# Order of the products on TensorE: second products alternate upper and lower weights, first products go 1, 3, 2, 4

## The chip, the cores and the metric

The kernel runs on one core of one Trainium2 chip. The metric is device time in microseconds (us) of one execution. Before the change the median of 3 runs is 1911.17 us (1909.87 to 1912.69).

## What is computed

An attention with 49 agents in the middle, followed by a two-layer network on every token. The inputs are `q`, `k`, `v` of 4 batches x 12480 tokens x 128, `agents` of 4 x 49 x 128, `w_in` of 128 x 2048 and `w_out` of 2048 x 128, all in double or single precision on the host's side.

```python
a2k = sm(agents, k)              # softmax(scale * agents @ k.T)
agent_v = a2k @ v                # 49 x 128 for each batch
q2a = sm(q, agents)              # tokens x 49
x = (q2a @ agent_v)              # the attention's output, 49920 tokens x 128
h = np.maximum(x @ w_in, 0.0)    # 49920 x 2048
out = h * h @ w_out              # 49920 x 128
```

## The kernel before

The network's first layer is folded into the attention: for each batch a table `aw` = `agent_v @ w_in` (49 rows, kept as an upper part `aw_hi` and a small remainder in `aw_ex`) is made, and the hidden layer of 480 tokens is then a product of `aw` with the softmax weights of these tokens (`w` and `x`). The 2048 hidden columns are cut into 16 chunks of 128. The unit of the main loop is a pair of two double chunks, that is four chunks of 128 columns for one group of 480 tokens; there are 416 such units, called pairs below. For each pair TensorE (PE) does this:

- Four **first products**, `h<-w,aw_hi`: the weights are four neighbouring pieces of 128 columns of `aw_hi`, and the moving operand is each time the same `w` (128 x 480). They write two tiles of PSUM, `hs[0]` and `hs[1]`, of two banks each. The pool `ps_h` has three such tiles, so `hs[0]` of a pair takes the tile that was `hs[1]` two pairs before, and `hs[1]` takes the tile that was `hs[0]` one pair before.
- Four small products, `h<-x,aw_ex`, 19 rows each, which add the remainder to the four outputs and run at the same time in four strips of the array.
- Up to sixteen small products of background work (`psa<-...`), which stand between the next four, in some pairs.
- Four products of the half-precision remainder `o<-g_lo,wo_half` and eight **second products** `o<-g_hi,wo_hi` and `o<-g_hi,wo_lo`, for the pair that came two before. All twelve add into one PSUM tile `o`. The eight take the four tiles `g_hi` (the squared hidden values, 128 x 480) each with an upper and a lower part of `w_out`.

Meanwhile ScalarE (ACT) takes `r` = relu of `hs[0]` and of `hs[1]` (two instructions, line 464) and squares both into `g_hi`. VectorE (DVE) multiplies `gg<-r,h` out of `hs[0]`, which is the last reader of `hs[0]`, then `h<-r,h` in place in `hs[1]` and `g_lo<-h,g_hi` out of it, which is the last reader of `hs[1]`. GpSimd (POOL) makes the other half of `g_lo` at line 493.

The order on PE, ACT and DVE is fixed by hand: the helper `queued` (line 464 is the call in it) chains each instruction behind the one issued before it on its engine. What comes first in the Python loops comes first on the engine. The background work of the next batch (scores, softmax, tables) is dealt out between these steps by `step` and `share`. The lines that the change touches are the loop over the four first products in `first` and the list `todo` in `second`.

Of the kernel before, what the change touches and what calls it, by code (L numbers as in the profile page):

```python
# [43 lines left out]
def agent_attention_relu2(ctx: ExitStack, tc: tile.TileContext, qT, kT, v, agT, w_in, w_out, outT):  # L44
    nc = tc.nc
# [35 lines left out]
    for base in (NA, -NA):  # L81
        nc.gpsimd.affine_select(
            out=quad.rearrange("p h a -> p (h a)"), in_=quad.rearrange("p h a -> p (h a)"),
# [4 lines left out]
    wo_hi = const.tile([P, NCH, C], F32R, name="wo_hi")  # L88
    wo_lo = const.tile([P, NCH, C], F32R, name="wo_lo")
# [106 lines left out]
    state = {}  # L196
# [264 lines left out]
    def queued(issue, eng, *args, **kw):  # L461

        with tc.issue_after(chain[eng]) if eng in chain else ExitStack():
            ins = issue(*args, **kw)  # L464
        chain[eng] = ins.ins
        return ins

    def first(k):

        g, i = divmod(k, SLOTS)  # L470
        j, c = divmod(i, NP)
        b = g // NB
        w, x = weights[g][j]
        hs = [ps_h.tile([P, 2, 512], F32, name="h") for _ in range(2)]
        outs = [h[:, n, :G] for h in hs for n in range(2)]
        for n, out in enumerate(outs):
            cs = slice((2 * c + n) * P, (2 * c + n + 1) * P)
            queued(nc.tensor.matmul, nc.tensor, out, state[b]["hi"][:, cs], w, start=True, stop=False)

        with tc.high_priority():  # L480
            for t, out in enumerate(outs):
                rows = slice(t * 32, t * 32 + NL)
                queued(nc.tensor.matmul, nc.tensor, out, state[b]["lo"][rows, c // 2, :], x[rows, :], start=False, stop=True)
        r = ffn.tile([P, 2, 2, G], F32, name="r", bufs=RB)
        hi = ffn.tile([P, 2, 2, G], F32R, name="g_hi", bufs=HB)
        gg = ffn.tile([P, 2, G], F32, name="gg", bufs=GB)
        queued(nc.scalar.activation, nc.scalar, r[:, 0], hs[0][:, :, :G], AF.Relu, scale=2.0**-26)
        queued(nc.vector.tensor_mul, nc.vector, gg, r[:, 0], hs[0][:, :, :G])
        queued(nc.scalar.activation, nc.scalar, r[:, 1], hs[1][:, :, :G], AF.Relu, scale=2.0**-26)
        queued(nc.scalar.activation, nc.scalar, hi, r, AF.Square, scale=2.0**13)  # L490
        lo = ffn.tile([P, 2, G], F16, name="g_lo", bufs=LB)
        for n in range(2):
            chain[nc.gpsimd] = nc.gpsimd.tensor_sub(lo[:, n, :], gg[:, n, :], hi[:, 0, n, :].bitcast(F32)).ins  # L493
        parts[k] = hi[:, 0], lo
        yield
        queued(nc.vector.tensor_mul, nc.vector, hs[1][:, :, :G], r[:, 1], hs[1][:, :, :G])
        yield
        lo = ffn.tile([P, 2, G], F16, name="g_lo", bufs=LB)
        queued(nc.vector.tensor_sub, nc.vector, lo, hs[1][:, :, :G], hi[:, 1].bitcast(F32))
        parts[k + 1] = hi[:, 1], lo  # L500
# [3 lines left out]
    def share(n, new):  # L504
        if n == 1:
            calls = [fill.pop(0) for _ in range(min(len(fill), NT // 2 if many[0] else NT))]
            due[:] = [[], [], [], []]
            for at in range(len(calls)):
                due[2 + at % 2 if new else 1 + at % 3].append(None)
            for d in due:  # L510
                for at in range(len(d)):
                    d[at] = calls.pop(0)
        for call in due[n]:
            call()
# [5 lines left out]
    def second(k):  # L520
        g, i = divmod(k, SLOTS)
        j, c = divmod(i, NP)
        if c == 0:
            acc[0] = ps_t.tile([P, 512], F32, name="o", tag=f"turn{turn[0]}")
        o = acc[0]
        pair = [(c + d, *parts.pop(k + d)) for d in range(2)]
        todo = [(wo_half[:, 2 * c + n, :], lo[:, n, :]) for c, hi, lo in reversed(pair) for n in range(2)]
        for c, hi, lo in pair:
            todo += [(w[:, 2 * c + n, :], hi[:, n, :]) for w in (wo_hi, wo_lo) for n in range(2)]
        for n, (w, y) in enumerate(todo):  # L530
            if 0 < n < 4:
                share(n, i % NP == 0)
            queued(
                nc.tensor.matmul, nc.tensor, o[:, :G], w, y,
                start=(i % NP == 0 and n == 0), stop=(c == NP - 1 and n == len(todo) - 1),
            )
        return (g, j, o) if c == NP - 1 else None
# [7 lines left out]
    def background(b):  # L545

        kt = load_keys(b, 0, kv, "kt")
        for i in range(NB):
            nxt = load_keys(b, i + 1, kv, "kt") if i + 1 < NB else load_values(b, 0, kv, "vt")
            yield from scores(b, i, kt)  # L550
            yield 0.5
            kt = nxt
        yield from maxima(b)
        yield
        vt = load_values(b, 1, kv, "vt")
        ready = yield from weighed(b, 0, kt, False, nc.gpsimd)
        for i in range(NB):
            yield PACE
            nxt = load_values(b, i + 2, kv, "vt") if i + 2 < NB else None
            more = (yield from weighed(b, i + 1, vt, False, nc.gpsimd)) if i + 1 < NB else None  # L560
            yield from gathered(b, i, *ready)
            vt, ready = nxt, more
        yield
        yield from tables(b)
# [73 lines left out]
    for k in range(total + LAG):  # L638
        if k < total:
            g, c = divmod(k, SLOTS)  # L640
            b, i = divmod(g, NB)
            if k > LAG and (k - LAG) % NP == 0:
                turn[0] = 1 - turn[0]
            if i == 0 and c == 0 and b + 1 < B:
                todo = background(b + 1)
# [26 lines left out]
            if k % 2 == 0:  # L672
                begun = first(k)
                next(begun)
        if k % 2 == 0:
            ready = second(k - LAG) if k >= LAG else flush()
            marks.append([chain[nc.scalar], chain[nc.vector], chain[nc.gpsimd]])
            next(begun, None)
            if ready:
                out(*ready)  # L680
        else:
            next(begun, None)
# [32 lines left out]
```

## Time and profile before

| | |
|---|---|
| median of 3 runs | 1911.17 us |
| lowest, highest | 1909.87, 1912.69 us |
| the profiled execution, its own time | 1909.7 us |
| its span, first to last instruction | 1907.9 us |
| mean granted TensorE clock | 0.991 |
| PE busy | 1872.2 us (98%) |
| ACT busy | 1677.9 us (88%) |
| DVE busy | 1659.8 us (87%) |
| POOL busy | 1354.4 us (71%) |

A busy share says how much of the span an engine had an instruction running. Matmuls are pipelined, so the records of one overlap those of the next: a matmul of 480 columns has a record of about 0.38 us, while the next starts about 0.2 us after it. What a matmul costs is therefore read from the distance of two starts, not from its duration. The weights of a matmul are loaded by a separate record (PEld), which runs while the matmul before it streams.

### The profile page before, as it was taken

The numbers are of one execution on the slowest core, as the hardware profiler recorded it, in microseconds if no ns is written. First come the engines' busy times: TensorE is split into PE (matmuls) and PEld (weight loads), VectorE is DVE, ScalarE is ACT, GpSimd is POOL, SyncE is SP. The second block draws the span as 40 slices with busy tenths as digits, with TensorE's granted clock in tenths as the row PEclk, the third lists the DMA queues.
The fourth block names the chain that finished last, engine by engine and source line by source line (L and its number), as shares of the span: only waits on it lengthen the run. The fifth ranks groups of instructions, "written<-read, shape, count | busy, mean of one in ns | idle before, by whom it ended". The sixth has DMA issues, their size and how long they took to land.

```text
span 1907.9 us, 31019 instructions
## 1 busy us (share of the span) xinstructions
PE 1872.2 (98%) x10778; PEld 1396.9 (73%) x10778; DVE 1659.8 (87%) x1936; ACT 1677.9 (88%) x1613; POOL 1354.4 (71%) x1288
## 2 busy tenths in 40 slices
PE   7799999999999999999999999999999999999999
PEld 7577777777777777777767877777767777777776
DVE  6987888888987888888998788888899989999897
ACT  3577899998887899999888789999889999999997
POOL 2665688987665688988666568989767676767675
PEclk8899999999999999999999999999999999999999
DMA  9343222221123322222112322222111111111110
GB/s 300 108 124 97 78 84 71 77 79 52 60 65 97 102 79 72 78 78 62 59 45 87 103 67 71 83 73 64 56 44 55 52 51 53 47 52 46 58 36 29
DMA packets 67025, 142.81 MB, mean 75 GB/s; under 512 B 9304, under 2 KB 45812, under 8 KB 66868
## 3 DMA queue, kind: packets, MB, share of 16 engines
q1 hardware_dynamic: 66868, 140.83, 24.4%
q8 instruction: 85, 1.39, 0.3%
q14 instruction: 72, 0.59, 0.1%
HBM read 81.17 MB, written 25.56 MB: 56 GB/s over the span
## 4 chain that ended last, share of the span: by engine, by line
PE 86%; DVE 6%; DMA 3%; issue 2%; ACT 2%; POOL 1%; SPq 0%; POOLq 0%; DVEq 0%; ACTq 0%
PE o L464 52%; PE h L464 24%; PE psa L464 10%; DVE gg L464 2%; DMA raw<-in_w_in 1%; DVE g_lo L464 1%; DMA ahead<-in_v 1%; ACT r L464 1%; DVE h L464 1%; POOL g_lo L493 1%; DVE aw_half L362 1%; ACT g_hi L464 1%; DMA ahead<-in_kT 0%; DMA raw<-in_w_out 0%; DVE ob L464 0%
## 5 line engine op out<-in xcount | busy, mean ns | idle before, releaser
L493 POOL TENSOR_TENSOR g_lo<-gg,g_hi 128x480 f16<-128x480 f32 x832 | 998.4, 1222 | 417.2 <-ACT g_hi L464 257.5
L464 ACT ACTIVATE r<-h 128x960 f32<-128x960 f32 x832 | 763.5, 967 | 117.5 <-PE h L464 59.8
L464 ACT ACTIVATE g_hi<-r 128x1920 fp32r<-128x1920 f32 x416 | 754.2, 1813 | 30.8 <-ACT r L464 1.1
L464 DVE TENSOR_TENSOR g_lo<-h,g_hi 128x960 f16<-128x960 f32 x416 | 479.9, 1154 | 124.9 <-ACT g_hi L464 95.1
L464 PE MATMUL o<-g_hi,wo_hi 128*128 128x480 f32 x1664 | 568.9, 423 | 0.0
L464 DVE TENSOR_TENSOR gg<-r,h 128x960 f32<-128x960 f32 x416 | 479.4, 1152 | 84.8 <-ACT r L464 80.0
L464 PE MATMUL o<-g_lo,wo_half 128*128 128x480 f16 x1664 | 516.8, 370 | 0.6 <-POOL g_lo L493 0.5
L464 PE MATMUL o<-g_hi,wo_lo 128*128 128x480 f32 x1664 | 495.9, 379 | 0.0
L464 DVE TENSOR_TENSOR h<-r,h 128x960 f32<-128x960 f32 x416 | 480.4, 1155 | 1.0
L464 PE MATMUL h<-w,aw_hi 128*128 128x480 f32 x1664 | 435.2, 382 | 12.4 <-DVE gg L464 5.1
L464 PEld LDWEIGHTS h<-w,aw_hi 128*128 128x128 f32 x1664 | 311.9, 189 | 69.2 <-DVE gg L464 13.1
L464 PEld LDWEIGHTS o<-g_hi,wo_hi 128*128 128x128 f32 x1664 | 314.6, 189 | 50.0 <-issue 0.8
L464 PEld LDWEIGHTS o<-g_hi,wo_lo 128*128 128x128 f32 x1664 | 312.5, 188 | 48.6
L464 PEld LDWEIGHTS <-wo_half 128*128 128x128 f16 x1664 | 172.0, 112 | 149.4 <-issue 97.0
L464 PE MATMUL h<-x,aw_ex 19*128 19x480 f16 x1664 | 159.5, 373 | 0.0
L464 PEld LDWEIGHTS <-aw_ex 19*128 19x128 f16 x1664 | 41.8, 91 | 138.7 <-issue 138.3
L464 PEld LDWEIGHTS psa<-ag,qt 128*120 128x120 f32 x816 | 127.6, 187 | 6.8 <-issue 0.4
L464 PE MATMUL psa<-ag,qt 128*120 128x49 f32 x816 | 118.2, 249 | 0.0
L398 POOL TENSOR_TENSOR e<-e,z 120x392 f32<-120x392 f32 x52 | 44.2, 850 | 60.9 <-PE h L464 33.8
L266 POOL TENSOR_TENSOR vs<-vt,vs 120x1024 fp32r<-120x1024 f32 x39 | 85.8, 2200 | 0.0
L464 PEld LDWEIGHTS psa<-ag,kt 128*120 128x120 f32 x624 | 78.1, 184 | 5.8 <-DVE ob L464 3.2
L464 PE MATMUL psa<-ag,kt 128*120 128x49 f32 x624 | 76.8, 260 | 0.1
(152 smaller groups left out, 1121.4 us busy)
## 6 DMA issues: line engine op xcount, KB each, us to landing
qt<-in_qT SPq DMA_DIRECT2D x52, 480.0 KB
out_T<-ob SPq DMA_DIRECT2D x104, 240.0 KB
vt<-in_v SPq DMA_DIRECT2D x39, 483.8 KB
kt<-in_kT SPq DMA_DIRECT2D x39, 480.0 KB
w<-ph SPq DMA_DIRECT2D x102, 91.9 KB
w<-y SPq DMA_DIRECT2D x102, 91.9 KB
x<-half SPq DMA_DIRECT2D x416, 17.8 KB
ahead<-in_v SPq DMA_DIRECT2D x13, 483.8 KB
```

Of the source, the lines that this page charges most:

```text
L266: last[nc.gpsimd] = nc.gpsimd.tensor_sub(vs[:, :, C + 1 : 2 * C + 1], vt[:, :, :C], vs[:, :, :C].bitcast(F32))
L362: cut = nc.vector.tensor_copy(half, lo.bitcast(F32)).ins
L398: nc.gpsimd.tensor_mul(e, e, z.broadcast_to([TP, NT, NA]))
L464: ins = issue(*args, **kw)
L493: chain[nc.gpsimd] = nc.gpsimd.tensor_sub(lo[:, n, :], gg[:, n, :], hi[:, 0, n, :].bitcast(F32)).ins
```

## The change

Two loops are written in another order. In `first` the four products of a pair are issued for `n` in 0, 2, 1, 3 and no longer 0, 1, 2, 3; each keeps its own weights and output. In `second` the eight products of a pair are issued as upper, lower on the first `g_hi` tile, then upper, lower on the next, and no longer upper on two tiles and then lower on the same two.

```diff
-        for n, out in enumerate(outs):
+        for n in (0, 2, 1, 3):
             cs = slice((2 * c + n) * P, (2 * c + n + 1) * P)
-            queued(nc.tensor.matmul, nc.tensor, out, state[b]["hi"][:, cs], w, start=True, stop=False)
+            queued(nc.tensor.matmul, nc.tensor, outs[n], state[b]["hi"][:, cs], w, start=True, stop=False)
...
-            todo += [(w[:, 2 * c + n, :], hi[:, n, :]) for w in (wo_hi, wo_lo) for n in range(2)]
+            todo += [(w[:, 2 * c + n, :], hi[:, n, :]) for n in range(2) for w in (wo_hi, wo_lo)]
```

On PE, early in the main loop, the second products of one pair and the first products of the next stand in this row before (`o` is the sum in PSUM; `h_1413` is `hs[0]` of the new pair and `h_1414` its `hs[1]`; what an instruction waits for stands in brackets):

```order
L464 MATMUL o_1240<-g_hi_1281,wo_hi_103 128x480 [waits Activation_49]
L464 MATMUL o_1240<-g_hi_1281,wo_hi_103 128x480
L464 MATMUL o_1240<-g_hi_1281,wo_lo_104 128x480 x2
L464 MATMUL o_1240<-g_hi_1281,wo_hi_103 128x480 x2
L464 MATMUL o_1240<-g_hi_1281,wo_lo_104 128x480 x2
L464 MATMUL h_1413<-w0_1150,aw_hi_764 128x480 [waits DVE_49]
L464 MATMUL h_1413<-w0_1150,aw_hi_764 128x480
L464 MATMUL h_1414<-w0_1150,aw_hi_764 128x480 [waits DVE_49]
L464 MATMUL h_1414<-w0_1150,aw_hi_764 128x480
```

And the same place on PE now:

```order
L464 MATMUL o_1240<-g_hi_1281,wo_hi_103 128x480 [waits Activation_49]
L464 MATMUL o_1240<-g_hi_1281,wo_lo_104 128x480
L464 MATMUL o_1240<-g_hi_1281,wo_hi_103 128x480
L464 MATMUL o_1240<-g_hi_1281,wo_lo_104 128x480
L464 MATMUL o_1240<-g_hi_1281,wo_hi_103 128x480
L464 MATMUL o_1240<-g_hi_1281,wo_lo_104 128x480
L464 MATMUL o_1240<-g_hi_1281,wo_hi_103 128x480
L464 MATMUL o_1240<-g_hi_1281,wo_lo_104 128x480
L464 MATMUL h_1413<-w0_1150,aw_hi_764 128x480 [waits DVE_49]
L464 MATMUL h_1414<-w0_1150,aw_hi_764 128x480 [waits DVE_49]
L464 MATMUL h_1413<-w0_1150,aw_hi_764 128x480
L464 MATMUL h_1414<-w0_1150,aw_hi_764 128x480
```

Upper and lower weights now alternate one by one, and the first write to `hs[1]`, with its wait for DVE, moved from the third place among the first products to the second.

The rows of ACT and SP are the same. On DVE and POOL only the first two or three pairs after the start differ, where the decoding of `w_out` (lines 117 and 118) and the first softmax (lines 388 to 397) are fitted between the pairs' steps. On DVE:

```order
-L464 TENSOR_TENSOR gg<-r,h 128x960
 L117 TENSOR_SCALAR rest<-raw 128x256
-L388 TENSOR_REDUCE m<-psa 120x8
+L118 SCALAR_TENSOR_TENSOR rest<-raw,rest 128x256
 L117 TENSOR_SCALAR rest<-raw 128x256
-L464 TENSOR_TENSOR h<-r,h 128x2x480
+L464 TENSOR_TENSOR gg<-r,h 128x960
 L118 SCALAR_TENSOR_TENSOR rest<-raw,rest 128x256
-L390 TENSOR_TENSOR e<-psa,m 120x392
```

There the first `gg` moved behind three steps of the decoding, and the softmax's `m` and `e` moved further back.

## Rows read from the trace of the kernel before

**Rows 1.** The profile's page: busy time of the engines, and the chain of work that ended last, its shares by engine and line.

```profile
PE 1872.2 (98%) x10778; PEld 1396.9 (73%) x10778; DVE 1659.8 (87%) x1936; ACT 1677.9 (88%) x1613; POOL 1354.4 (71%) x1288
...
PE o L464 52%; PE h L464 24%; PE psa L464 10%; DVE gg L464 2%; DMA raw<-in_w_in 1%; DVE g_lo L464 1%; DMA ahead<-in_v 1%; ACT r L464 1%; DVE h L464 1%; POOL g_lo L493 1%; DVE aw_half L362 1%; ACT g_hi L464 1%; DMA ahead<-in_kT 0%; DMA raw<-in_w_out 0%; DVE ob L464 0%
```

**Rows 2.** The group of the first products among PE's matmuls: count, busy us and mean ns of one record, and PE's idle time before them with what ended it.

```profile
L464 PE MATMUL h<-w,aw_hi 128*128 128x480 f32 x1664 | 435.2, 382 | 12.4 <-DVE gg L464 5.1 <-DVE aw_lo L357 3.8 <-issue 3.3
```

**Rows 3.** PE in order of time through two pairs without background work: start in us, time from the first start to the last end of the merged records, and their count.

```profile
1565.43 0.38 PE L464 MATMUL h<-x,aw_ex 19*128 19x480 f16 x4
1565.74 0.98 PE L464 MATMUL o<-g_lo,wo_half 128*128 128x480 f16 x4
...
1567.00 0.60 PE L464 MATMUL o<-g_hi,wo_lo 128*128 128x480 f32 x2
1567.43 0.59 PE L464 MATMUL o<-g_hi,wo_hi 128*128 128x480 f32 x2
1567.86 0.60 PE L464 MATMUL o<-g_hi,wo_lo 128*128 128x480 f32 x2
1568.30 1.03 PE L464 MATMUL h<-w,aw_hi 128*128 128x480 f32 x4
1569.26 0.38 PE L464 MATMUL h<-x,aw_ex 19*128 19x480 f16 x4
...
1572.12 0.38 PE L464 MATMUL h<-w,aw_hi 128*128 128x480 f32 x1
```

**Rows 4.** The same view in windows so narrow that single products can be told apart: the first and the last of four first products, the last of four half-precision products, and the later one of each two second products.

```profile
1564.47 0.38 PE L464 MATMUL h<-w,aw_hi 128*128 128x480 f32 x1
...
1565.12 0.37 PE L464 MATMUL h<-w,aw_hi 128*128 128x480 f32 x1
...
1566.36 0.37 PE L464 MATMUL o<-g_lo,wo_half 128*128 128x480 f16 x1
...
1567.22 0.38 PE L464 MATMUL o<-g_hi,wo_lo 128*128 128x480 f32 x1
...
1567.65 0.38 PE L464 MATMUL o<-g_hi,wo_hi 128*128 128x480 f32 x1
...
1568.08 0.38 PE L464 MATMUL o<-g_hi,wo_lo 128*128 128x480 f32 x1
```

**Rows 5.** PE's weight loads: the groups over the whole span (count, busy us, mean ns of one, idle before), and one load in order of time beside the rows above.

```profile
L464 PEld LDWEIGHTS o<-g_hi,wo_hi 128*128 128x128 f32 x1664 | 314.6, 189 | 50.0 <-issue 0.8
L464 PEld LDWEIGHTS o<-g_hi,wo_lo 128*128 128x128 f32 x1664 | 312.5, 188 | 48.6
L464 PEld LDWEIGHTS h<-w,aw_hi 128*128 128x128 f32 x1664 | 311.9, 189 | 69.2 <-DVE gg L464 13.1 <-DVE aw_lo L357 5.1 <-issue 3.9
...
1567.00 0.19 PEld L464 LDWEIGHTS o<-g_hi,wo_lo 128*128 128x128 f32 x1
```

**Rows 6.** All engines in order of time at a pair in which PE waits for `gg` of the pair before (the brackets hold the idle time before a record and what ended it).

```profile
1441.39 1.13 DVE L464 TENSOR_TENSOR gg<-r,h 128x960 f32<-128x960 f32 x1
...
1441.81 0.59 PE L464 MATMUL h<-w,aw_hi 128*128 128x480 f32 x2
...
1442.58 0.30 PEld L464 LDWEIGHTS h<-w,aw_hi 128*128 128x128 f32 x2 [0.58 <-DVE gg L464]
1442.58 0.70 PE L464 MATMUL h<-w,aw_hi 128*128 128x480 f32 x2 [0.17 <-DVE gg L464]
...
1443.22 0.38 PE L464 MATMUL h<-x,aw_ex 19*128 19x480 f16 x4
```

**Rows 7.** Who waited for whom, PE's weight loads: us in total, times, longest.

```profile
PEld h L464 <- DVE gg L464: 13.1, 23, 1.7
```

**Rows 8.** DVE and PE in order of time at two pairs in which `gg` comes late but PE does not wait yet, from the last batch; the second lies ten blocks of eight pairs after the first.

```profile
1522.80 1.15 DVE L464 TENSOR_TENSOR gg<-r,h 128x960 f32<-128x960 f32 x1
...
1523.74 1.03 PE L464 MATMUL h<-w,aw_hi 128*128 128x480 f32 x4
...
1846.84 1.15 DVE L464 TENSOR_TENSOR gg<-r,h 128x960 f32<-128x960 f32 x1
...
1847.79 1.03 PE L464 MATMUL h<-w,aw_hi 128*128 128x480 f32 x4
```

**Rows 9.** The same view at a pair where `gg` is only a little late.

```profile
1583.86 1.15 DVE L464 TENSOR_TENSOR gg<-r,h 128x960 f32<-128x960 f32 x1
...
1584.94 1.03 PE L464 MATMUL h<-w,aw_hi 128*128 128x480 f32 x4
```

**Rows 10.** The same view at the first and at the last pair after the start where `gg` ends later than the first of the first products starts by more than 0.06 us; 63 of the 416 pairs are such.

```profile
232.84 1.15 DVE L464 TENSOR_TENSOR gg<-r,h 128x960 f32<-128x960 f32 x1 [0.72 <-ACT r L464]
...
232.91 0.59 PE L464 MATMUL h<-w,aw_hi 128*128 128x480 f32 x2
...
1885.57 1.15 DVE L464 TENSOR_TENSOR gg<-r,h 128x960 f32<-128x960 f32 x1 [0.35 <-POOL g_lo L493]
...
1886.52 1.03 PE L464 MATMUL h<-w,aw_hi 128*128 128x480 f32 x4
```

**Rows 11.** PE in order of time at the first pair of the main loop.

```profile
81.29 0.70 PE L464 MATMUL h<-w,aw_hi 128*128 128x480 f32 x2 [1.78 <-DVE aw_lo L357]
84.05 0.96 PE L464 MATMUL h<-w,aw_hi 128*128 128x480 f32 x2 [2.05 <-DVE aw_lo L357]
```

## The prediction

> **What bounds the kernel now.** The page comes first: PE is busy for 98% of the span, and the chain that ended last lies on PE's lines `o`, `h` and `psa` for 86% of it [rows 1]. So the time is the sum of PE's steps, plus the moments in which PE waits. ACT and DVE, at 88% and 87%, have room, but little. Then the timeline of two pairs without background work shows what the steps are. A pair starts at 1568.30 and the next at 1572.12, that is 3.82 us [rows 3]. The first products start 0.65 us apart over three steps (1564.47 to 1565.12), 0.217 us each [rows 4]; the last six steps of the second products up to the next pair take 1568.30 - 1567.00 = 1.30 us, also 0.217 us each [rows 3]; the half-precision ones take 0.62 us for three (1565.74 to 1566.36), 0.207 us each [rows 3, 4]. All have 480 columns, so the single-precision ones are not paced by their columns. The weight loads say by what: a load takes 188 or 189 ns whichever tensor it reads, and it starts with the matmul before it, since a load and a matmul stand at 1567.00 both [rows 3, 5]. 0.188 us of load and some 0.028 us around it are the step of 0.217. Last come PE's waits. The first products have 12.4 us of idle time before them, of which 5.1 us ended with `gg` on DVE [rows 2]; seen at the weight loads it is 23 waits for `gg` and 13.1 us [rows 7]. The reader is to keep two things: a step is a weight load plus a fixed rest, and what the first products wait for most often is `gg` of the pair before, which frees the tile that becomes `hs[1]`.
>
> **Part one, second products.** Nothing is added or removed: the same eight loads and eight matmuls, on the same bank. What changes is which load runs beside which stream. Before, the moving operand changes at every step; now it stays for the lower weights. The first products show a stream that stays, 0.217 us a step, and the second ones a stream that changes, 0.217 us a step [rows 3, 4]. So I take 0 for this part. To the nanosecond the steps are not all alike. Worked out from the same records of all 413 pairs that are complete (one is shown, from 1567.00 to 1568.30 [rows 3], with single starts [rows 4]), a step to a neighbouring piece of weights has a median of 218 ns, and a step that jumps from `wo_hi` to `wo_lo` or back 215 ns: 0.22, 0.21, 0.22, 0.21 at the page's resolution. First products, all neighbours, have 218 to 219. But in the second products a neighbour's step is also always one from the first to the second tile of `g_hi`, so the 3 ns can hang on the weights or on the moving operand. If on the operand, the reordering moves them about and gains nothing. If on the weights, four steps of a pair fall by 3 ns. If a stream that stays is what costs the first products 218 to 219, against a mean of 217 for the second, four steps rise by up to 2 ns. Per pair that is -12 to +8 ns, times 416 pairs -5.0 to +3.3 us. I take 0, since the load's record is as long for neighbours (`h`, 189 ns) as for the others (188 and 189 ns) [rows 5]: an effect of where the weights lie should be seen in the load.
>
> That agrees with the Trainium skill, in "SBUF — State Buffer", section "Who interferes with whom": TensorE has two read ports into SBUF, one for the moving operand and one for weights, and they are independent. By that rule a new pairing of stream and load is worth 0; the 3 ns in the trace show that the rule does not explain every step, and no run here shows on which side they arise.
>
> **Part two, first products.** The order 1, 3, 2, 4 takes the neighbouring weights apart: by the weights' account three steps of a pair fall by 3 ns, -9 ns x 416 = -3.7 us; by the other account 0, which I take for the same reason.
>
> The other half of this edit is the wait. The first write to `hs[1]` moves from third to second, so it asks for the tile 0.22 us earlier. It waits for `gg` of the pair before. What is queued behind it are all later products of PE, then ACT's `r`, which cannot start before the small products have completed the tile. How early must `gg` end? At the waiting pair, `gg` ends at 1441.39 + 1.13 = 1442.52, the load begins at 1442.58, and of the two products that follow, 0.70 us in all, the last record of 0.38 us starts at 1442.90; less one step of 0.22, the product that waited really began at 1442.68, 0.16 us after `gg`'s end [rows 6]. Before the change this product's turn is 0.44 us after the first one's start F, so PE loses nothing while `gg` ends before F + 0.28. Now its turn is at F + 0.22, and `gg` must end before F + 0.06. A pair whose `gg` ends later than F + 0.06 loses the difference, but at most 0.22 us, because beyond F + 0.28 PE waited before too and now merely has three products left to do behind the wait and not two.
>
> At the waiting pair F is 1441.81 and `gg` ends 0.71 us after it: a full 0.22. At two pairs of the last batch [rows 8], 1522.80 + 1.15 = 1523.95 against F = 1523.74 is 0.21 late, and 1846.84 + 1.15 = 1847.99 against 1847.79 is 0.20 late: they lose 0.14 to 0.15, where today they lose nothing. At another [rows 9] it is 1585.01 against 1584.94, 0.07: a loss of 0.01. Such pairs after the start number 63, from F = 232.91 to F = 1886.52 [rows 10], and the formula added over them, each with its own `gg` and F, gives 7.7 us. In some places late pairs follow each other; there PE's delay in the first gives the second that much slack. Carried on from pair to pair: 15 pairs lose the full 0.22 (3.3 us), 7 followers and partly late ones lose 0.9 us, 14 pairs of the kind of [rows 8] lose 1.9 us, and the small ones as in [rows 9] lose 0.3 us. Together 6.4 us. As a check from another view, 23 waits for `gg` [rows 7] x 0.22 us = 5.1 us, for those that are stalls today. None of it is hidden: PE is busy for 98% of the span [rows 1] and has next to nothing to give outside such waits, so a step that it starts late ends the span late.
>
> **The start.** In the first pair `hs[1]` comes free late as well: the second half of the first products starts at 84.05, the first at 81.29 [rows 11]. One more product behind that wait is 0.2 us. DVE's steps there are reshuffled, the first `gg` goes behind three decoding steps; the work is the same and PE waits for it either way. I take 0, with a bound of 1 us either way.
>
> **Sum.** 0 + 0 + 6.4 + 0.2 = 6.6 us. The profiled execution took 1909.7 us, 1907.9 of it the span, so its counterpart would be 1916.3. The median of the runs is 1.5 us above that execution, and on it the sum gives 1917.8 us, 0.34% more.
>
> **The rivals.** About 0.2%, 3.8 us, is what a measurement here can tell from no change.
>
> First, on the other side: *neighbouring weights cost 3 ns.* For it speaks that every 218 in the records is a step to a neighbour and every 215 a jump, and that after the change no load reads the piece behind the last one. Then seven steps of a pair fall by 3 ns: 21 x 416 = 8.7 us, less the 6.6 of the waits, -2.1 us: 1909. It decides in favour of faster by over 0.2% from 10.4 us on, that is 25 ns a pair, which needs 3.6 ns for each of the seven steps, or smaller waits. If the steps came down to the 0.207 us of the half-precision products it would be far more, 7 x 10 ns x 416 = 29 us and 1889, but a load of 188 ns and its rest stand against that. Chance 0.27, half of it faster.
>
> Second, *the waits are given back*: `gg` comes earlier after a delay of PE, because ACT and DVE catch up, so that the next late pair is less late than in the trace. Where ACT is the late one, this is already in the sum; if it held at all 63 pairs, 2 to 3 us would be left: 1914, no change that can be told. Chance 0.13.
>
> Third, *a stream that stays costs more*: +3.3 us for part one on top of the waits, 1921. The first products' 218 to 219 speak for it, though they differ in more than that. Chance 0.15.
>
> **How the numbers follow.** The forecast, waits of 6.6 us and steps unchanged, has 0.45: 1917.8, with 1914.5 to 1920 as its own range; a tenth of it lies below 0.2%. Faster by over 0.2%: half of the first rival, 0.14. Within 0.2%: the other half, 0.13, with 0.10 of the second and 0.04 of the forecast, 0.27. Slower: 0.41 of the forecast, 0.15 of the third, 0.03 of the second, 0.59. The range reaches down to 1907.5, which takes in most of the first rival, and up to 1922, the third with its share of the start.
>
> **What would show it.** In the new profile the weight loads of `h` should wait for `gg` oftener than 23 times and the idle time before the first products, 12.4 us on PE, should rise by 1 to 4 us with more of it put down to `gg`; where PE waits, three products should stand behind the wait and one ahead. In a quiet pair 3.82 us should stay, and three second-product steps should still take 0.65 us. A quiet pair of 3.80 us would show the first rival, one of 3.83 the third. A pair like that at 1847.79 that runs on without a wait would show the forecast wrong.

## The result and the profile after

The changed kernel takes 1921.64 us, the median of 6 runs (1920.17 to 1923.44), against 1910.78 us for the kernel before, also 6 runs. The ratio is 1.0055, with a 95% interval of 1.0045 to 1.0066: 10.9 us slower. The profiled execution took 1920.17 us, its span 1918.4 us, 10.5 us more than the span before. Of all executions of the runs below one, of "wait alone", took 2054.66 us at a granted clock of 0.838, where the others show about 0.99; it is left out of that run's median.

First the page of the changed kernel: busy time, and the chain that ended last by line.

```profile
PE 1877.0 (98%) x10778; PEld 1393.5 (73%) x10778; DVE 1664.9 (87%) x1936; ACT 1678.3 (87%) x1613; POOL 1352.0 (70%) x1288
...
PE o L464 50%; PE h L464 24%; PE psa L464 9%; DVE gg L464 2%; DMA ahead<-in_v 1%; DVE g_lo L464 1%; ACT r L464 1%; DVE h L464 1%; POOL g_lo L493 1%; DVE aw_half L362 1%; DMA ahead<-in_kT 1%; DVE ob L464 0%; ACT g_hi L464 0%; DMA raw<-in_w_in 0%; PE h L194 0%
```

It hardly differs from [rows 1]: no engine changed its work and PE is the bound as it was. The loss has to be looked for in PE's idle time and in the distance of its starts. The group of the first products:

```profile
L464 PE MATMUL h<-w,aw_hi 128*128 128x480 f32 x1664 | 440.3, 384 | 15.6 <-DVE gg L464 8.7 <-DVE aw_lo L357 3.2 <-issue 3.2
```

and who waited for whom, PE's weight loads:

```profile
PEld h L464 <- DVE gg L464: 21.0, 37, 2.4
```

The idle time before the first products rose from 12.4 to 15.6 us [rows 2]; what is put down to `gg` rose from 5.1 to 8.7 us, more than the whole. And 37 weight loads wait for `gg` where 23 did [rows 7]. The same pair as in [rows 6], all engines in order of time:

```profile
1449.04 1.14 DVE L464 TENSOR_TENSOR gg<-r,h 128x960 f32<-128x960 f32 x1
...
1449.49 0.38 PE L464 MATMUL h<-w,aw_hi 128*128 128x480 f32 x1
...
1450.23 0.52 PEld L464 LDWEIGHTS h<-w,aw_hi 128*128 128x128 f32 x3 [0.76 <-DVE gg L464]
1450.23 0.92 PE L464 MATMUL h<-w,aw_hi 128*128 128x480 f32 x3 [0.36 <-DVE gg L464]
...
1451.09 0.38 PE L464 MATMUL h<-x,aw_ex 19*128 19x480 f16 x4
```

One product stands ahead of the wait and three behind it. From the end of `gg` (1449.04 + 1.14 = 1450.18) to the small products are 0.91 us; before it was 1443.22 - 1442.52 = 0.70 us. That is the one step of 0.21 us more behind the wait. It is the rule and not this pair alone: over all loads that wait for `gg`, the median time from the end of `gg` to the small products is 0.69 us before (23 waits) and 0.91 us now (37 waits). The second pair of [rows 8], where PE did not wait before, now does:

```profile
1856.87 1.14 DVE L464 TENSOR_TENSOR gg<-r,h 128x960 f32<-128x960 f32 x1
...
1857.87 1.13 PE L464 MATMUL h<-w,aw_hi 128*128 128x480 f32 x4
...
1858.07 0.52 PEld L464 LDWEIGHTS h<-w,aw_hi 128*128 128x128 f32 x3 [0.23 <-DVE gg L464]
...
1858.93 0.38 PE L464 MATMUL h<-x,aw_ex 19*128 19x480 f16 x4
```

From the first product to the small ones are 1.06 us. In the quiet pair of [rows 3], quiet meaning without background work, they are 1569.26 - 1568.30 = 0.96. By the prediction's formula this pair loses 0.08 us here (`gg` ends at 1858.01, 0.14 after the first product starts, less 0.06).

PE through the same quiet pairs as in [rows 3]:

```profile
1573.04 1.04 PE L464 MATMUL h<-w,aw_hi 128*128 128x480 f32 x4
1574.01 0.38 PE L464 MATMUL h<-x,aw_ex 19*128 19x480 f16 x4
...
1575.36 0.38 PE L464 MATMUL o<-g_hi,wo_lo 128*128 128x480 f32 x1
1575.58 0.38 PE L464 MATMUL o<-g_hi,wo_hi 128*128 128x480 f32 x1
...
1576.88 1.04 PE L464 MATMUL h<-w,aw_hi 128*128 128x480 f32 x4
...
1580.72 0.60 PE L464 MATMUL h<-w,aw_hi 128*128 128x480 f32 x2
```

A pair takes (1580.72 - 1573.04) / 2 = 3.84 us, and not 3.82 as from 1568.30 to 1572.12; over all 156 pairs without background work the median went from 3.827 to 3.840 us. And the start, where in [rows 11] the first products began at 81.29 and 84.05:

```profile
81.83 0.48 PE L464 MATMUL h<-w,aw_hi 128*128 128x480 f32 x1 [0.95 <-DVE aw_lo L357]
84.58 1.57 PE L464 MATMUL h<-w,aw_hi 128*128 128x480 f32 x3 [2.27 <-DVE aw_lo L357]
...
91.74 1.57 PE L464 MATMUL h<-w,aw_hi 128*128 128x480 f32 x3 [1.17 <-DVE gg L464]
...
110.50 1.03 PE L464 MATMUL h<-w,aw_hi 128*128 128x480 f32 x4
```

The last row is the fifth pair. In the trace of before it stands here:

```profile
107.04 1.03 PE L464 MATMUL h<-w,aw_hi 128*128 128x480 f32 x4
```

On DVE, the first `gg` and what runs just ahead of it, first before, then in the changed kernel:

```profile
87.34 0.89 DVE L362 CAST aw_half<-aw_lo 49x512 f16<-49x512 f32 x1
88.16 1.14 DVE L464 TENSOR_TENSOR gg<-r,h 128x960 f32<-128x960 f32 x1
...
87.89 0.89 DVE L362 CAST aw_half<-aw_lo 49x512 f16<-49x512 f32 x1
88.71 0.28 DVE L117 TENSOR_SCALAR rest<-raw 128x256 uint32<-128x256 uint32 x1
89.02 0.85 DVE L118 SCALAR_TENSOR_TENSOR rest<-raw,rest 128x256 f32<-128x256 uint32 x1
89.80 0.83 DVE L117 TENSOR_SCALAR rest<-raw 128x256 uint32<-128x256 uint32 x1
90.54 1.14 DVE L464 TENSOR_TENSOR gg<-r,h 128x960 f32<-128x960 f32 x1
```

The step of line 362 starts 0.55 us later than before, which is the later start of the first product (81.83 against 81.29). `gg` follows it at once before; now three decoding steps stand between, and it starts 90.54 - 88.16 = 2.38 us later. TensorE's granted clock is lower for longer as well: from 98 to 100 us it is 0.50 (1.2 GHz) in the changed kernel, with PE busy for 0.33 us of these two, and 1.00 (2.4 GHz) before, with PE busy throughout.

So three things are seen in the traces: more waiting, longer quiet pairs, and a later start. For the runs below each is measured by its own stretch. The *lead* is the time of the very first product; it lies between 81.0 and 84.3 us in the thirteen profiled executions, in no order that follows the kernel. The *start* goes from there to the fifth pair. The *body* goes from the ninth pair to the last. Its two ends, before and then in the changed kernel:

```profile
126.78 0.38 PE L464 MATMUL h<-w,aw_hi 128*128 128x480 f32 x1
...
1894.18 0.38 PE L464 MATMUL h<-w,aw_hi 128*128 128x480 f32 x1
...
130.25 0.38 PE L464 MATMUL h<-w,aw_hi 128*128 128x480 f32 x1
...
1904.62 0.38 PE L464 MATMUL h<-w,aw_hi 128*128 128x480 f32 x1
```

Before: start 25.75, body 1767.40. After: start 28.68, body 1774.37, that is +2.9 and +7.0 us.

### The profile page after: what moved, and what is told of

It is laid out like the page before. It is cut to its first block, busy times and chain, and to the rows that moved or that the text cites. A ratio compares the mean times of both kernels' runs of the same rounds, so it can differ in the third digit from the quotient of the medians.

```text
span 1918.4 us, 31020 instructions
## 1 busy us (share of the span) xinstructions
PE 1877.0 (98%) x10778; PEld 1393.5 (73%) x10778; DVE 1664.9 (87%) x1936; ACT 1678.3 (87%) x1613; POOL 1352.0 (70%) x1288
## 4 chain that ended last, share of the span: by engine, by line
PE 84%; DVE 8%; issue 3%; DMA 3%; ACT 2%; POOL 1%; SPq 0%; POOLq 0%; DVEq 0%; ACTq 0%
PE o L464 50%; PE h L464 24%; PE psa L464 9%; DVE gg L464 2%; DMA ahead<-in_v 1%; DVE g_lo L464 1%; ACT r L464 1%; DVE h L464 1%; POOL g_lo L493 1%; DVE aw_half L362 1%; DMA ahead<-in_kT 1%; DVE ob L464 0%; ACT g_hi L464 0%; DMA raw<-in_w_in 0%; PE h L194 0%
## 5 line engine op out<-in xcount | busy, mean ns | idle before, releaser
L464 PE MATMUL o<-g_hi,wo_hi 128*128 128x480 f32 x1664 | 704.2, 423 | 0.0
L464 PE MATMUL o<-g_hi,wo_lo 128*128 128x480 f32 x1664 | 631.5, 380 | 0.0
L464 PE MATMUL h<-w,aw_hi 128*128 128x480 f32 x1664 | 440.3, 384 | 15.6 <-DVE gg L464 8.7
```

## The experiments

Eleven kernels were run. Times are medians, set against the kernel before on the same chip (1910.1 to 1910.2 us). None leaves work out. Start, body and waits are read from one profiled execution each. The body of "weights apart" is 0.9 us longer than before although its steps and waits are the same, so a difference of this size says nothing by itself.

| run | time, us | ratio, 95% interval | start, us | body, us | waits for `gg` | quiet pair, us |
|---|---|---|---|---|---|---|
| before | | | 25.75 | 1767.40 | 23 | 3.827 |
| the change | 1921.64 | 1.0055 (1.0045 to 1.0066) | 28.68 | 1774.37 | 37 | 3.840 |
| second only | 1914.33 | 1.0021 (1.0013 to 1.0030) | 25.70 | 1770.13 | 23 | 3.840 |
| first only | 1920.34 | 1.0045 (1.0032 to 1.0057) | 28.64 | 1773.08 | 49 | 3.827 |
| start as before | 1917.50 | 1.0037 (1.0023 to 1.0051) | 25.81 | 1774.56 | 37 | 3.840 |
| weights apart | 1911.37 | 1.0005 (0.9996 to 1.0013) | 25.70 | 1768.29 | 22 | 3.827 |
| "wait first" | 1910.61 | 1.0001 (0.9992 to 1.0010) | 25.71 | 1767.58 | 23 | 3.827 |
| cross | 1910.49 | 0.9997 (0.9988 to 1.0006) | 25.85 | 1767.30 | 22 | 3.827 |
| half alternating | 1911.43 | 1.0004 (0.9995 to 1.0013) | 25.83 | 1768.20 | 22 | 3.833 |
| two between | 1910.94 | 1.0007 (0.9998 to 1.0015) | 25.39 | 1768.12 | 22 | |
| more behind the wait | 1948.28 | 1.0196 (1.0182 to 1.0211) | 25.37 | 1805.74 | 129 | |
| wait alone | 1916.19 | 1.0029 (1.0017 to 1.0040) | 25.83 | 1773.00 | 50 | 3.827 |
| last half | 1918.20 | 1.0036 (1.0023 to 1.0049) | 25.84 | 1773.95 | 21 | 3.854 |

**The second products alone.**

```diff
-            todo += [... for w in (wo_hi, wo_lo) for n in range(2)]
+            todo += [... for n in range(2) for w in (wo_hi, wo_lo)]
```

> Only the second products alternate upper and lower; the first products keep their order. My reading of the two traces (the change costs by three items: the earlier wait for gg about 4 us, the reshuffled start about 3 us, the steps themselves about 3 us, of which 1.4 us in the second products) gives +1.4 us over the kernel before, no difference that can be told, with the waits of the weight loads for gg back at about 23 and the start as before. The rival that a stream that stays is the main cost gives +3 us or more, with mean steps of the second products above 0.218 us. The rival that neighbouring weights cost 3 ns gives -4 to -5 us.

The body is 2.7 us longer and the waits are as before. PE's first products at the quiet pairs:

```profile
1567.90 1.04 PE L464 MATMUL h<-w,aw_hi 128*128 128x480 f32 x4
1568.87 0.38 PE L464 MATMUL h<-x,aw_ex 19*128 19x480 f16 x4
1571.74 1.04 PE L464 MATMUL h<-w,aw_hi 128*128 128x480 f32 x4
...
1575.58 0.38 PE L464 MATMUL h<-w,aw_hi 128*128 128x480 f32 x1
```

The 3.84 us of the changed kernel are here, and so are the 0.97 us from the first product to the small ones (1568.87 - 1567.90) in place of 0.96, although the first products stand in the old order. So my 1.4 us was too little: I had put the longer step to the small products on the first products' account, and it belongs to the second ones. The whole lengthening of the quiet pair is theirs. The time itself is 4.3 us longer (2.5 to 5.7 by the interval), with 1.6 us of the profiled execution's loss in the lead; the body's 2.7 us is the part that the trace shows behind the start.

**The first products alone.**

```diff
-        for n, out in enumerate(outs):
+        for n in (0, 2, 1, 3):
```

> Only the first products go 1, 3, 2, 4. My reading: nearly the whole loss is here, +9 to +9.5 us: waits for gg about 4 us, start about 3 us, and about 2 us from the small products behind, which begin 312 ns and no longer 308 ns after the last first product. About 37 waits of the weight loads for gg. The rival that the second products carry most of it gives +5 us or less.

The body is 5.7 us longer, the start 2.9 us, and a quiet pair is what it was, 3.827 us. The order 1, 3, 2, 4 moves no step's mean by over 0.5 ns, over pairs without a wait; all it costs are waits and the start.

**The start as before.** This is the whole change, but with the old order of the first products in the first four pairs.

```diff
-        for n in (0, 2, 1, 3):
+        for n in ((0, 1, 2, 3) if k < 8 else (0, 2, 1, 3)):
```

> The whole change, but the first four pairs keep the old order of the first products, so that the scheduler's order on DVE at the start is that of before. If the reshuffled start costs what the trace shows (the fifth pair starts 3.5 us later than before, 0.5 us of it before the first product), the time falls by 3 us against the whole change, to about +8 us over the kernel before, and the fifth pair starts within 1 us of 107.0 us. If the start's delay is only what waits for gg cost there anyhow, or the runs vary that much there, the time stays at +10 to +11 us.

The fifth pair in order of time on PE:

```profile
107.55 1.04 PE L464 MATMUL h<-w,aw_hi 128*128 128x480 f32 x4
```

The start is 25.81 us again and the time falls from 1921.64 to 1917.50. DVE's order at the start is that of before here, so both what reshuffles it and the first waits are gone; the 2.9 us are the start's, and this run does not part the two. The granted clock is 0.50 from 98 to 100 us here too, and the start is not longer for it, so a low clock up to there is not the cost.

**Weights apart, wait where it was.** The second and the third chunk of every four change places in the tiles: weights are read 1, 3, 2, 4, tiles written 1, 2, 3, 4.

```diff
+TURN = (0, 2, 1, 3)
...
-            cs = slice((2 * c + n) * P, (2 * c + n + 1) * P)
+            cs = slice((2 * c + TURN[n]) * P, (2 * c + TURN[n] + 1) * P)
...
-            for t, out in enumerate(outs):
+            for t, out in enumerate(outs[n] for n in TURN):
```

> The second and third chunk of every four change places in the tiles, so that the first products read their weights in the order 1, 3, 2, 4 but write the two tiles in the old order, with the wait in the third place; the second products keep upper, upper, lower, lower and take each weight where it belongs. My reading: the wait is where it was, so 0 of the 4 us; the time is that of before within 2 us. The rival that neighbouring weights cost 3 ns a step gives -3.7 us at the first products and the same again at the second ones. If the longer step to the small products comes from the order of the weights, +1.8 us; if from the order of the banks, none.

The time is that of before. Weights that do not lie next to each other gain nothing, with which the first rival falls.

**The wait first, as I meant it.**

```diff
-        for n, out in enumerate(outs):
+        for n in (2, 3, 0, 1):
```

> A bigger dose of the wait: the first products go 3, 4, 1, 2, so that the tile which gg frees is asked for by the very first of them, one place earlier than in the change and two earlier than before; the second products are those of before. If the wait is what the order 1, 3, 2, 4 costs, a pair loses up to 0.43 us now: the formula of the prediction added over the trace of before gives 19.8 us, against 7.6 us for the second place, of which 5.7 us were measured with the first products alone; in that proportion +15 us here (12 to 18), and more than 60 waits of weight loads for gg. If the cost is in the order of banks or weights instead, +9 us or less.

Nothing happened, and the trace shows why at the pair of [rows 6]:

```profile
1441.83 0.59 PE L464 MATMUL h<-w,aw_hi 128*128 128x480 f32 x2
...
1442.59 0.70 PE L464 MATMUL h<-w,aw_hi 128*128 128x480 f32 x2 [0.17 <-DVE gg L464]
```

Two products still run ahead of the wait. This fits that whichever of the two tiles is written first takes the place in PSUM that came free first, so that the edit changed names and not the wait; the places themselves are not shown in the profile. The run therefore says nothing of the wait's price; it shows that turning the weights about costs nothing either.

**Cross: weights alternate, streams too.**

```diff
-            todo += [(w[:, 2 * c + n, :], hi[:, n, :]) for w in (wo_hi, wo_lo) for n in range(2)]
+        pieces = [(2 * c + n, hi[:, n, :]) for c, hi, lo in pair for n in range(2)]
+        for turn_ in range(2):
+            todo += [((wo_hi, wo_lo)[(turn_ + t) % 2][:, at, :], y) for t, (at, y) in enumerate(pieces)]
```

> Second products on alternating upper and lower weights, but never twice on the same moving operand: upper on tiles 1 and 3 with lower on 2 and 4, then the other way round. If a stream that stays is what makes the steps longer, the time is that of before within 1.5 us, a pair without background work takes 3.827 us and the small products follow 0.307 us after the last first product. If alternating the weights does it, +3 to +4 us as in the run with the second products alone, with 3.840 us and 0.312 us.

The time is that of before, and so is the mean of every step over pairs without a wait, to within 0.2 ns. PE in order of time:

```profile
1565.67 1.02 PE L464 MATMUL h<-w,aw_hi 128*128 128x480 f32 x4
1566.63 0.38 PE L464 MATMUL h<-x,aw_ex 19*128 19x480 f16 x4
...
1573.32 0.38 PE L464 MATMUL h<-w,aw_hi 128*128 128x480 f32 x1
```

(1573.32 - 1565.67) / 2 is 3.825 us. Alternating upper and lower weights costs nothing by itself. What costs comes with the order in which the moving operand stays for two products. In all orders tried these two products also take the upper and the lower piece of the same chunk of `w_out` one right behind the other, and no run parts the two.

The run also answers a question of the prediction: the steps of 215 and 218 ns stand in the same places here, although every step but the middle one now goes from upper to lower or back, and every step changes the operand. In both orders the 218 are the steps from the first to the second `g_hi` tile of a double chunk, and "weights apart" has them too, whose second products never take two neighbouring weights in a row. So the 3 ns do not hang on the weights; operand and place in the row are not parted.

**Half alternating, and last half.** The first four, or the last four, of the eight alternate on a staying operand.

```diff
+        PLAIN = [(w, n) for w in (wo_hi, wo_lo) for n in range(2)]
+        ALT = [(w, n) for n in range(2) for w in (wo_hi, wo_lo)]
...
+            todo += [... for w, n in (ALT if hi is pair[0][1] else PLAIN)]
```

(The other run has `PLAIN if hi is pair[0][1] else ALT`.)

> Of the eight second products the first four alternate upper and lower on one moving operand, the last four stay as before. If each pair of products on one stream costs its share, half of the longer second products remains (about 1.5 ns a pair) and the time is +1 to +2 us. If the longer steps of the first and the small products (about 5 ns a pair) come from how the second products before them end, these go back to 0.307 us between the last first product and the small ones; if they come from the alternation anywhere, they stay at 0.312 us.

> The mirror of the run in which the first four second products alternate: here the last four do, on one moving operand each two. If the longer step to the small products (0.312 us) is set by how the second products before it end, it is back here, with about 5 ns a pair of it, and the time is +2 to +3 us; if each two products on one stream cost the same wherever they stand, the pair is 6 to 7 ns longer as a whole and the time is +1 to +1.5 us.

The bodies are 0.8 and 6.6 us longer; all eight together cost 2.7. The 0.8 is no more than the 0.9 by which "weights apart" differs from before with equal steps; only the quiet pair of 3.833 us shows a cost there. So the costs do not add up, and for the last half both theories put on record missed it. PE's quiet pairs in "last half":

```profile
1569.38 1.03 PE L464 MATMUL h<-w,aw_hi 128*128 128x480 f32 x4
1570.34 0.38 PE L464 MATMUL h<-x,aw_ex 19*128 19x480 f16 x4
...
1577.09 0.38 PE L464 MATMUL h<-w,aw_hi 128*128 128x480 f32 x1
```

(1577.09 - 1569.38) / 2 = 3.855 us a pair. Here the step to the small products was not the long one (its mean over pairs without a wait 0.308 us, against 0.307 before and 0.312 with all eight), so that two products on one operand at the end of the second products do not by themselves set it either.

**Two second products between.** The wait's turn was to come 0.43 us later.

```diff
+            if n == 2:
+                while held:
+                    held.pop(0)()
...
+            if n >= len(todo) - 2 and c != NP - 1 and k + LAG + 2 < total:
+                held.append(call)
```

> The other direction: the kernel before, but the last two second products of a pair (not of the last pair of a group of four) stand between the second and the third first product of the next pair, so that the product that waits for gg has its turn 0.43 us later. By the wait's account the stalls that are there before the change shrink: the formula gives 5.5 us saved over all pairs, a quarter of which have nothing moved, so -4 us (-2.5 to -5.5) and at most 15 waits of weight loads for gg. If such stalls are given back elsewhere, by ACT or DVE which become the bound, the time stays within 1.5 us of before.

No gain. The way from one `gg` to the next is a ring: the small products end, `r`, `gg`, the waiting product, the products behind it, the small products. Of PE's work, 4 half-precision, 8 second and 2 first products lie in it ahead of the wait with or without this edit. Only their order changed. My 4 us forgot that the pair's small products move with the row. By itself this run fits the other reading on record as well, that ACT or DVE take the gain away; the next run is the one that speaks for the ring.

**More behind the wait.** The same two second products, now behind the waiting product, with the order 1, 3, 2, 4 from the fifth pair on.

```diff
+        for at, n in enumerate((0, 1, 2, 3) if k < 8 else (0, 2, 1, 3)):
+            if at == 2:
+                while held:
+                    held.pop(0)()
```

> First products 1, 3, 2, 4 from the fifth pair on, and two second products of the pair before (not at the end of a group of four) put behind the product that waits for gg. Between the wait and the small products, which start the way to the next gg, PE now has five products and not three, before the change two. If what counts is PE's work in that closed way and not the place in the row, a pair loses up to 0.65 us against before instead of 0.22; the formula with its limit moved by 0.43 us, carried from pair to pair, gives 36 us for all pairs, three quarters of them affected: +25 us (18 to 32), and well over 60 waits of weight loads for gg. If only the place among the first products counts, it is as with the order 1, 3, 2, 4 alone, +5 to +6 us.

The pair of [rows 6] in order of time:

```profile
1464.92 1.13 DVE L465 TENSOR_TENSOR gg<-r,h 128x960 f32<-128x960 f32 x1
...
1465.14 0.45 PE L465 MATMUL h<-w,aw_hi 128*128 128x480 f32 x1
...
1466.11 0.49 PE L465 MATMUL h<-w,aw_hi 128*128 128x480 f32 x1 [0.52 <-DVE gg L465]
...
1466.44 0.60 PE L465 MATMUL o<-g_hi,wo_lo 128*128 128x480 f32 x2
...
1466.87 0.59 PE L465 MATMUL h<-w,aw_hi 128*128 128x480 f32 x2
1467.39 0.38 PE L465 MATMUL h<-x,aw_ex 19*128 19x480 f16 x4
```

From the end of `gg` (1466.05) to the small products are 1.34 us, which is also the median over the 129 waits; it was 0.70 before and 0.91 with the order 1, 3, 2, 4.

The waits of the weight loads:

```profile
PEld h L465 <- DVE gg L465: 60.8, 129, 1.9
```

+38 us, more than the 18 to 32 expected, with 129 waits. The waiting product stands in the second place as in "wait alone", which lost 5.6 us of body; so PE's work between the wait and the small products is what costs, and the place among the first products is only the change's way of setting it. That it is more than the formula gives fits many pairs that are now late one after the other, where no slack is handed on, but that was not tried apart.

**The wait alone.** First products 1, 3, 2, 4 from the fifth pair on, everything else as before.

```diff
-        for n, out in enumerate(outs):
+        for n in ((0, 1, 2, 3) if k < 8 else (0, 2, 1, 3)):
```

> The first products 1, 3, 2, 4 from the fifth pair on, the first four pairs and all second products as before. With the start and the steps left alone only the earlier wait is left: +5.5 us (4 to 6.5), a pair without background work at 3.827 us, and 40 to 50 waits of weight loads for gg. If the start and the steps were the whole loss of the first-products run, 0 to +2 us.

The waits of the weight loads:

```profile
PEld h L464 <- DVE gg L464: 21.3, 50, 1.5
```

The body is 5.6 us longer with unchanged steps and an unchanged start, and 50 loads wait for `gg`, with a median of 0.91 us from its end to the small products.

## Why the prediction was right, and where its sum was off

The direction and the main mechanism were right. The time, 1921.64, lies just inside the range, which ended at 1922; the forecast of +6.6 us was 4.3 us short of the measured +10.9, and its own range, 1914.5 to 1920, missed the time. That the whole range held is in part luck: its upper end was made for the third rival, which had a chance of 0.15, and that rival's 1921 comes so close while it leaves out the start. By its steps:

- **The wait at the second place**, 6.4 us: alone it measures 5.6 us in the body ("wait alone"). The reading that made it, three products behind the wait and not two, stands in the rows, and the run with more behind the wait shows it by a bigger dose. The text put it as "its turn is 0.22 us earlier"; the runs "two between" and "more behind the wait" show that the better words are how much of PE's work lies between the wait and the small products. For this change both give the same number.
- **The second products**, taken as 0 with -5.0 to +3.3 us as bounds: 2.7 us. The size is that of the third rival, "a stream that stays costs more", with its +3.3, and it came on top of the waits as that rival had it. It is not spread as the rival had it: of four staying couples three have a step that can be read in quiet pairs, and these take 221, 215 and 215 ns; over half of the loss, 7 of 12 ns a quiet pair, lies in the step from the last first product to the small ones, where no second product takes part. I chose 0 because the weight loads' records are equally long, and this argument fails: it speaks against the weights' account only, and the loads stay at 0.19 us while the steps change. The cross run takes the cost off the alternation of the weights. I had named the row that pointed there, the first products' 218 to 219 ns on one operand, and gave it 0.15.
- **The weights' account**, the first rival: refuted twice. "Weights apart" and the first products alone leave the steps as they were.
- **A step as a load plus a fixed rest**: not shown. In the trace of before, four background products of 49 columns with a load each:

```profile
1443.53 0.61 PEld L464 LDWEIGHTS psa<-ag,qt 128*120 128x120 f32 x4
1443.74 0.52 PE L464 MATMUL psa<-ag,qt 128*120 128x49 f32 x4
1444.10 0.37 PE L464 MATMUL o<-g_lo,wo_half 128*128 128x480 f16 x1
```

  Their loads have records of 187 ns in the mean, as long as those of the second products, yet the four take 1444.10 - 1443.74 = 0.36 us, 0.09 each. So the length of a load's record is no lower bound of a step, and that the loads set the 0.217 us does not follow. The half-precision products of 480 columns, at 0.207 us, lie so close to it that the columns may set both; no run tries it. The sum does not use this reading, but one of the reasons for 0 rested on it.
- **The start**, 0.2 us with a bound of 1 us either way: 2.9 us. This is the term that was mis-sized most. I argued that the reshuffled DVE steps are the same work and that PE waits for them either way. But `gg` is waited for there while the decoding steps are not yet, so their order matters: the first `gg` starts at 90.54 on DVE where it started at 88.16, 1.84 us later when the later lead is taken off, and the second pair waits 1.17 us for it. These 1.84 us are DVE's order: in both traces the step of line 362 holds DVE equally long after the first product, and only the three decoding steps come between. The one more product behind the wait costs more than the 0.2 us, too: from the later first products to the small ones are 86.09 - 84.58 = 1.51 us, before 84.94 - 84.05 = 0.89, but `gg` did not start by that much later because DVE was busy anyhow. How the 2.9 us of all four pairs divide is open; with both undone all of it is gone.
- **The sum.** 2.9 + 5.6 + 2.7 = 11.2 us, the parts from one trace each. The change's start and body lost 9.9 in its trace. By the times the two halves alone lose 4.3 and 10.3 us and together 10.9, so they do not simply add. The body lost 7.0, not 5.6 + 2.7: with the longer pairs `gg` ends earlier in PE's terms, and 37 loads wait instead of 50. This is read from the counts, not tried apart.
- **"The waits are given back"**, the second rival: hardly, with the wait alone: the formula over all 63 pairs gave 7.7 us, with the slack carried on 6.4, and 5.6 were measured. Beside the changed second products 7.0 - 2.7 = 4.3 us are left for the waits, so some of that time is given back there.
- **The rule on the read ports.** The Trainium skill, in "SBUF — State Buffer", section "Who interferes with whom", has the two read ports of TensorE independent, and I took it as one more reason for 0. For where the weights lie the runs agree: 1768.29 against 1767.40 us of body in "weights apart", with equal steps. That a staying operand costs 2.7 us is not explained by it.

What stays open is why a staying operand costs what it does. By the body, two of four such couples cost 0.8 us where they come first and 6.6 us where they come last, and four cost 2.7. The first products stay on one operand for four products, and their steps did not change with their order. The differences are a few ns a step and reach into steps of other products that come after.

## What to carry to other kernels

Where one engine is the bound and waits for another once in each round, count the bound engine's work that lies between that wait and the instruction that starts the other engine's next round: an instruction moved in there is paid at each late round, in full where the round waits anyhow and in part where it is only a little late. Moving instructions about outside that stretch gained nothing in the one run that tried it. Price such an edit by the slack of each round in the trace, not by the few stalls that the profile shows today: here 23 waits before, but 63 rounds within reach. And when a scheduler fills in work from another stage, compare its order at the start too: three reshuffled steps made the first `gg` 1.84 us later here.

## What was not expected of the hardware

- The order in which moving operands come shifts the distance of matmuls by a few ns with the same loads and the same columns: quiet pairs of 3.827, 3.833, 3.840 and 3.854 us for four orders of the same eight products. Part of it shows in later products that were not touched: the step from the last first product to the small ones is 0.307 us before and 0.312 us when the second products alternate.
- Where the weights lie in SBUF and whether they neighbour each other showed no effect on these products, with loads of 0.19 us: the steps before and in "weights apart", "wait first" and "cross" are the same to within 0.2 ns in the mean over pairs without a wait.
- The product that had to wait has its record begin with its own load (both at 1450.23), so that a wait looks 0.1 us shorter on PE than it is: from there to the small products are 0.86 us, and the same three steps of a quiet pair take 0.74. The distance from the end of `gg` to the small products, as used above, does not depend on that record.
